# Decode attention block on one core: part of the K and V loads issued from ScalarE's queue

## The chip, the core and the metric

The kernel runs on one core of a Trainium2 chip. The core has five engines with a queue of instructions each: TensorE (PE, matrix products; PEld are its weight loads), VectorE (DVE), ScalarE (ACT), GpSimd (POOL) and SyncE (SP), which here only issues transfers. 16 DMA engines move data from the chip's memory (HBM) to the on-chip buffer (SBUF, 128 partitions). A transfer is issued by an instruction in the queue of SP, ACT or POOL, which first waits until the destination is free. The metric is the device time of the kernel in microseconds, the median of the runs; lower is better.

## What is computed

One decode step for a batch of 2, model width 512: layer norm, attention of 32 heads of width 128 over 8192 cached keys and values (float32), output projection with residual, then layer norm and an MLP (1792 wide, gelu) with residual. Cut to what matters:

```python
def _A_ref(x, k_cache, v_cache, wq, wo):     # x: (2, 1, 512)
    q = heads(x @ wq)                        # k_cache, v_cache: (2, 32, 8192, 128)
    scores = einsum("bhqd,bhkd->bhqk", q, k_cache) * 128 ** -0.5
    p = softmax(scores)
    o = einsum("bhqk,bhkd->bhqd", p, v_cache)
    return merge(o) @ wo
h = x + _A_ref(layernorm(x), k_cache, v_cache, wq, wo)
return h + mlp(layernorm(h), w1, b1, w2, b2)
```

K and V are 268 MB each, so nearly all of the bytes that the kernel reads are these two caches, each read once.

## The kernel before

The main loop runs over `NI` = 32 iterations: `i` stands for a pair of heads `m = i // 2` and a batch entry `b = i % 2`. Per iteration there is one load of K and one of V, 8.39 MB each: 128 partitions (64 for each of the two heads) with 128 consecutive cache rows, 64 KB, in each partition. `load` (line 70) issues them. Iterations 30 and 31 cut their loads into parts.

Three large buffers of 64 KB per partition (`kv`, `BUFS` = 3) hold the query weights at first, then K and V in turn, and at the end the MLP's weights. While one K is worked on, a V is being read or awaited, and the third buffer is filled.

Work on one K, in four chunks of 32 rows: VectorE multiplies the chunk by the query (`multiply`, line 246); GpSimd adds the upper half of 22 to 32 rows to the lower half (`halve`, line 256; in the last three iterations 12 in the last chunk and more shares for ScalarE); VectorE sums the rows to scores (`sums`, line 266). Only in the last three iterations does ScalarE sum rows (`by_act`, line 260). Then comes the maximum: `row_max` (line 270) on VectorE, a transpose on PE (273), `all_max` (277, 280), and on ScalarE `exps`: `nb` (286) and two exponentials (291). With these, PE multiplies V in 64 matmuls (`values`, line 314), ScalarE copies the result (`gather`, line 320) and PE sums it per head (`head_sum`, line 335). This second half, for iteration `i-1`, runs in iteration `i`, beside the chunks of K of `i`.

Order of the issues on SP. In iteration `i`, V of `i` is issued at the top, ahead of `all_max` and `exps` of `i-1`; K of `i+1` is issued after `values` of `i-1`. Each waits until the earlier contents of its buffer are no longer needed. Loads count from 0: K of `i` is load `2i` and V of `i` is load `2i+1`, up to iteration 29.

The output weights `wo` come in ten groups (`PLAN`): five as plain loads on SP (`load_wo`, line 140), and five as indirect loads issued by POOL (line 145), of 96 partitions with 8 KB each, which leave out blocks of partitions. `behind(m)` and `tc.issue_after` put an instruction behind another one in its engine's queue. ScalarE issues one transfer, the input `x` (line 66).

Of the kernel before, what the change touches and what calls it, by code (L numbers as in the profile page):

```python
# [9 lines left out]
F32 = mybir.dt.float32  # L10
I32 = mybir.dt.int32
BF16 = mybir.dt.bfloat16
AF = mybir.ActivationFunctionType
# [3 lines left out]
P = 128  # L17
# [8 lines left out]
BUFS = 3  # L26
# [11 lines left out]
FAR = 4096  # L38


@with_exitstack
def tile_decode_block(ctx: ExitStack, tc: tile.TileContext, x, k, v, wq, wo, w1, b1, w2, b2, out):
    nc = tc.nc
    B, H, SK, DH = k.shape
# [3 lines left out]
    NS = SK // HP  # L48
    NC = NS // CH
    DC = D // P  # L50
# [3 lines left out]
    NI = NM * B  # L54
    SCALE = DH ** -0.5
# [3 lines left out]
    kv = ctx.enter_context(tc.tile_pool(name="kv", bufs=BUFS))  # L59
# [7 lines left out]

    def load(src, i, parts):  # L70
        m, b = divmod(i, B)
        t = kv.tile([P, NS, DH], F32, name="kv", tag="kv")
        rows = src[b, QG * m:QG * m + QG].rearrange("h (p j) d -> (h p) j d", j=NS)
        for s0, n in parts:
            nc.sync.dma_start(t[:, s0:s0 + n], rows[:, s0:s0 + n])
        return t

    wqt = kv.tile([P, DC, H * DH], F32, name="wqs", tag="kv")
    nc.sync.dma_start(wqt, wq.rearrange("(p r) n -> p r n", r=DC))

    ident = const.tile([P, P], F32, name="ident")
# [13 lines left out]
    for blocks in PLAN:  # L95
        shut = blocks if isinstance(blocks, tuple) else None
        r = WR if shut else blocks
        n = (P - 4 * len(shut or ())) * r
# [13 lines left out]
    for _, _, _, blocks in groups:  # L112
        if blocks and blocks not in index:
# [3 lines left out]
            for p in sorted(set(ends)):  # L117
                if ends.count(p) == 1:
                    if p in blocks:
                        edge, step, first = p, FAR, p  # L120
                    else:
                        edge, step = p, first - p - FAR
                    one = work.tile([P, 1], F32, name="ix1")
# [11 lines left out]
    def load_wo(g, gate=None):  # L135
        r0, n, r, shut = groups[g]
        t = wts.tile([P, WR, D], F32, name="wog")
        wo_g[g] = t
        if not shut:
            nc.sync.dma_start(t[:, :r], wo[r0:r0 + n, :].rearrange("(p r) n -> p r n", r=r))  # L140
            return
        if gate is not None:
            next_of_pool(lambda: nc.gpsimd.tensor_copy(gate0, gate))
        next_of_pool(lambda: nc.gpsimd.memset(t, 0.0))
        next_of_pool(lambda: nc.gpsimd.indirect_dma_start(
            t.rearrange("p r n -> p (r n)"), None, wo_runs, bass.IndirectOffsetOnAxis(index[shut], 0),
            element_offset=r0 * D, bounds_check=n // r - 1, oob_is_err=False))
# [30 lines left out]
    ptz = [pt2[:, j] for j in range(2)]  # L178
# [9 lines left out]
    so2 = [psa.tile([P, 512], F32, name=f"so{j}") for j in range(2)]  # L188
# [49 lines left out]
    ST, MX, MT, GM, GI, LT, RL, SS, OP, TP = {}, {}, {}, {}, {}, {}, {}, {}, {}, {}  # L238
    wl = q2.rearrange("p (e n) -> p e n", e=QG)

    def multiply(i, c):
        if c == 0:
            ST[i] = work.tile([P, NS], F32, name="s", bufs=3)
        qb = qps[i // B][:, i % B, None, :].to_broadcast([P, CH, DH])
        kc = kt[i][:, c * CH:(c + 1) * CH, :]
        return nc.vector.tensor_tensor(kc, kc, qb, op=ALU.mult)  # L246
# [28 lines left out]
    def all_max(i):  # L275
        gm = work.tile([1, QG], F32, name="gm")
        last = nc.vector.tensor_reduce(gm, MT.pop(i).rearrange("o (e p) -> o e p", e=QG), axis=AX.X, op=ALU.max,  # L277
                                       negate=True)
        GM[i] = psm.tile([P, QG], F32, name="sm")
        GI[i] = nc.tensor.matmul(GM[i], ones[:1, :], gm, start=True, stop=True)  # L280
        return last

    def exps(i):
        m, b = divmod(i, B)
        nb = work.tile([P, QG], F32, name="nb")
        nc.scalar.activation(nb, GM.pop(i), AF.Copy, scale=SCALE)  # L286
        LT[m] = lt2[:, m % 2]
        s = ST.pop(i).rearrange("p (u j) -> p u j", j=4)
        for e in range(QG):
            ps = slice(e * HP, (e + 1) * HP)  # L290
            nc.scalar.activation(ptz[i % 2][ps, :, 4 * e:4 * e + 4], s[ps], AF.Exp, bias=nb[ps, e:e + 1], scale=SCALE,  # L291
                                 accum_out=LT[m][ps, 32 * e + b:32 * e + b + 1])

    def total(i):
        m, b = divmod(i, B)
# [14 lines left out]
    def values(i, us=range(NS // 4)):  # L310
        so = so2[i % 2]
        for u in us:
            n = u % NG
            m = nc.tensor.matmul(so[32 * n:32 * n + 4 * QG], ptz[i % 2][:, u, :], vt[i][:, 4 * u:4 * u + 4, :],  # L314
                                 start=(u < NG), stop=(u >= NS // 4 - NG))
        return m

    def gather(i):
        SS[i] = work.tile([P, 512], F32, name="ss", bufs=3)
        return nc.scalar.activation(SS[i], so2[i % 2], AF.Copy)  # L320

    def head_sum(i):
        m, b = divmod(i, B)
# [46 lines left out]
    def behind(m):  # L370
        return tc.issue_after(m.ins)
# [8 lines left out]
    def cut(n):  # L380
        return [(j * NS // n, NS // n) for j in range(n)]

    parts_of = {NI - 2: cut(2), NI - 1: cut(2)}
    kt, vt = {}, {}
    next_load = 0
    free_from = 1
    kt[0] = load(k, 0, cut(1))
    for i in range(NI):
        m, b = divmod(i, B)
        done = i - 1  # L390
        late = i == NI - 1
        if not late:
            if i < NI - 2:
                vt[i] = load(v, i, cut(1))
        else:
            vt[i] = load(v, i, [(0, 64), (64, 32), (96, 24), (120, 8)])
            b1r = rows2[:, 0].rearrange("p r q -> p (r q)")[:, :FN]
            nc.vector.memset(b1r, 0.0)
            b2s = rows2[:B, 1].rearrange("b r q -> b (r q)")
            for e in range(B):  # L400
                nc.sync.dma_start(b1r[WB * e::32], b1.rearrange("(n f) -> n f", n=NG))
            nc.sync.dma_start(b2s, b2[None, :].to_broadcast([B, D]))
        if i > 0:
            last = all_max(done)
            exps(done)
            if not late:
                values(done)
        if i < NI - 1:
            kt[i + 1] = load(k, i + 1, parts_of.get(i + 1, cut(1)))
        if i == NI - 2:  # L410
            vt[i] = load(v, i, cut(1))
            nc.sync.dma_start(wl, wo[HL * DH:, :].rearrange("(h p) n -> p h n", p=P))
        if next_load < len(groups) and i == free_from:
            load_wo(next_load, MX[i - 1][:1, 0:1] if next_load == 0 else None)
            next_load += 1
            free_from = NI
        for c in range(NC):
            if i > 0 and c == 0:
                with behind(last):
                    mul = multiply(i, c)  # L420
            else:
                mul = multiply(i, c)
            ended = [g for g in group_end.get(done // B, ())] if done >= 0 and done % B == B - 1 else []
            with behind(mul):
                if i > 0 and c == 1:
                    inverse(done)
                if i > 0 and c == 2 and done % B == B - 1:
                    for h in range(done // B * QG, done // B * QG + QG):
                        head_out(h)
                if c == 3:  # L430
                    for g in ended:
                        turned(g)
                        free_from = i + 1
            halve(i, c)
            by_act(i, c)
            if i > 0 and c == 0 and not late:
                gather(done)
            with behind(mul):
                if c > 0:
                    sums(i, c - 1, True)  # L440
                sums(i, c, False)
            if late and c == 1:
                spare = psq.tile([P, 512], F32, name="spare", tag="qps")
                awake = stay_awake(8, ST[i][:, :NPOOL[True][0]])
            if i > 0 and c == 0:
                total(done)
            if i > 0 and c == 1 and not late:
                head_sum(done)
            if c == 2:
                for g in ended:  # L450
                    turn(g)
        sums(i, NC - 1, True)
        if b == B - 1 and m % 2 == 1 and m + 1 < NM:
            make_q(m + 1)
        if late:
            with behind(awake):
                last = values(done, range(MOST))
            with behind(last):
                row_max(i)
        else:  # L460
            row_max(i)

    hl = NI - 1
    wt = kv.tile([P, 2, NS * DH // 2], F32, name="ws", tag="kv")
    w1t = wt[:, 0, :DC * F].rearrange("p (c f) -> p c f", c=DC)
    w1v = w1.rearrange("(p c) f -> p c f", c=DC)
    for c in range(0, DC, 2):
# [119 lines left out]
    for c in range(DC):  # L587
        with behind(last):
            for n in range(NG):
                m = nc.tensor.matmul(  # L590
                    pf[32 * n:32 * n + 32], cen[:, c, :], w1t[:, c, n * FN:(n + 1) * FN],
                    start=(c == 0), stop=(c == DC - 1))
# [58 lines left out]
```

## Time and profile before

| what | value |
|---|---|
| median of 3 runs | 1307.79 us (1307.79 to 1307.81) |
| span of the profiled execution | 1305.9 us, so 1.9 us of the median lie around it |
| busy: DVE / POOL / PE / ACT | 932.7 / 494.2 / 446.8 / 98.6 us |
| moved by DMA | 561.50 MB, mean 430 GB/s |
| busy share of the 16 DMA engines by slices | 9 (90% or more) in 39 of 40, 8 in the last |
| one multiply (line 246) | 4415 ns mean, 128 of them |

How to read the rows: in a timeline a row is the start in us, the duration in us, the engine and line, the operation, the tile written and the tiles read, the count, and in brackets how long the engine was idle before and what ended that. "SPq" and "ACTq" are the queues' own instructions, such as DMA issues. A row of waits is the waiting engine and line, whom it waited for, the total in us, how many times, and the longest. A row of DMA issues ends with the median time from the issue to the landing. In a row of windows the columns are the window, its length, then the busy time (and count) of PE, PEld, DVE, ACT and POOL, then the granted PE clock, the share of the DMA engines, and GB/s. A row of DMA queues is the queue, its packets, MB, and the share of the 16 engines' span. In the chain of waits, a row is start, duration and what the time went to.

### The profile page before, as it was taken

The page shows a single profiled execution, that of the slowest core. Times are in us where ns is not written, and L with a number is a line of the kernel's source. Part 1 is how long each engine was busy: PE and PEld are TensorE (multiplying, and loading weights), DVE is VectorE, ACT ScalarE, POOL GpSimd, SP SyncE. Part 2 cuts the span into 40 slices and gives each one's busy share as a digit, 9 for nine tenths or more (in the row PEclk, how much of TensorE's full clock was granted, in tenths as well). Part 3 has the DMA queues.
Part 4 walks back from the last instruction along what each step waited for, and adds up shares of the span by engine and source line. Part 5 has one row for each costly group of instructions (what it writes and reads, how often), then busy time and mean ns, then how long its engine had stood idle before and what let it go on. Part 6 is the DMA issues. An engine that isn't in the chain of part 4 may idle for free.

```text
span 1305.9 us, 7466 instructions
## 1 busy us (share of the span) xinstructions
PE 446.8 (34%) x2934; PEld 130.9 (10%) x2934; DVE 932.7 (71%) x551; ACT 98.6 (8%) x431; POOL 494.2 (38%) x151
## 2 busy tenths in 40 slices
PE   3033313333332334413342232333323334123468
PEld 0001001010010101001010010101001011000113
DVE  3666688757688666787766787666787667797891
ACT  0000000000000000000000000000000000004440
POOL 0433344532344432444332454333444433453330
PEclk9566556766566666656766566666666666566689
DMA  9999999999999999999999999999999999999998
GB/s 418 426 440 428 438 422 444 424 440 426 442 426 440 428 438 428 426 444 430 436 426 438 430 434 436 424 442 424 440 426 432 438 432 436 429 428 429 428 434 351
DMA packets 12727, 561.50 MB, mean 430 GB/s; under 512 B 1568, under 2 KB 1584, under 8 KB 2484
## 3 DMA queue, kind: packets, MB, share of 16 engines
q1 hardware_dynamic: 11968, 557.08, 98.8%
q0 software_dynamic: 720, 3.93, 0.7%
q8 instruction: 23, 0.38, 0.1%
q14 instruction: 12, 0.10, 0.0%
q10 hardware_dynamic: 4, 0.00, 0.0%
HBM read 562.32 MB, written 0.00 MB: 431 GB/s over the span
## 4 chain that ended last, share of the span: by engine, by line
DMA 43%; DVE 24%; issue 14%; PE 12%; POOL 5%; ACT 1%; SPq 0%; POOLq 0%; DVEq 0%
DMA kv<-in_A_k_cache_dram 38%; DVE kv L246 14%; PE so L314 10%; DVE s L266 9%; POOL kv L256 5%; DMA kv<-in_A_v_cache_dram 3%; DMA ws<-in_B_w_dram 1%; ACT pt L291 1%; PE rowacc L367 1%; DVE orow L350 1%; PE sm L280 1%; PE sm L273 0%; DVE gm L277 0%; DVE mx L270 0%; ACT nb L286 0%
## 5 line engine op out<-in xcount | busy, mean ns | idle before, releaser
L246 DVE TENSOR_TENSOR kv<-kv,qps 128x4096 f32<-128x4096 f32 x128 | 562.4, 4415 | 313.8 <-DMA kv<-in_A_k_cache_dram 313.6
L256 POOL TENSOR_TENSOR kv<-kv 128x2048 f32<-128x2048 f32 (+3 forms) x128 | 476.8, 3734 | 754.1 <-DVE kv L246 566.3
L266 DVE TENSOR_REDUCE s<-kv 128x32 f32<-128x2048 f32 (+5 forms) x160 | 325.3, 2066 | 10.9 <-POOL kv L256 10.6
L314 PE MATMUL so<-kv,pt 128*8 128x512 f32 x2048 | 280.8, 709 | 42.7 <-ACT pt L291 37.3
L273 PE MATMUL sm<-ident,mx 128*1 128x128 f32 x32 | 10.9, 340 | 446.0 <-DVE mx L270 446.0
L314 PEld LDWEIGHTS so<-kv,pt 128*8 128x8 f32 x2048 | 56.4, 101 | 239.5 <-issue 194.3
L367 PE MATMUL rowacc<-wog,ot 128*2 128x512 f32 x70 | 50.3, 881 | 64.8 <-DVE ot L365 33.4
L286 ACT ACTIVATE nb<-sm 128x2 f32<-128x2 f32 x32 | 5.5, 172 | 851.4 <-PE sm L280 851.4
L231 PE MATMUL qps<-q,pick 2*64 2x256 f32 x64 | 13.8, 577 | 127.6 <-DVE kv L246 127.6
L273 PEld LDWEIGHTS sm<-ident,mx 128*1 128x1 f32 x32 | 2.5, 79 | 472.5 <-issue 278.0
L358 PE MATMUL sm<-ident,orow 2*128 2x2 f32 x35 | 5.2, 244 | 130.1 <-DVE orow L350 130.1
L320 ACT ACTIVATE ss<-so 128x512 f32<-128x512 f32 x31 | 18.5, 598 | 269.6 <-PE so L314 269.6
L260 ACT ACTIVATE kv<-kv 128x128 f32<-128x128 f32 x114 | 33.5, 295 | 24.2 <-DVE kv L246 21.4
L335 PE MATMUL sm<-ss,selr 128*34 128x128 f32 x240 | 28.7, 273 | 0.0
L291 ACT ACTIVATE pt<-s,nb 64x128 f32<-64x128 f32 x64 | 25.5, 399 | 1.4
L335 PEld LDWEIGHTS sm<-ss,selr 128*34 128x34 f32 x240 | 25.1, 112 | 0.0
L260 ACT ACTIVATION_READ_ACCUMULATOR kv<-kv 128x1 f32 x114 | 21.3, 186 | 0.0
L280 PE MATMUL sm<-gm,ones 1*128 1x2 f32 x64 | 16.6, 326 | 11.9 <-DVE gm L277 11.9
L277 DVE TENSOR_REDUCE gm<-sm 1x2 f32<-1x128 f32 x32 | 8.9, 279 | 16.2 <-PE sm L273 16.2
L231 PEld LDWEIGHTS qps<-q,pick 2*64 2x64 f32 x64 | 5.5, 192 | 136.9 <-DVE kv L246 133.2
L358 PEld LDWEIGHTS sm<-ident,orow 2*128 2x128 f32 x35 | 4.4, 207 | 132.6 <-DVE orow L350 79.9
L367 PEld LDWEIGHTS rowacc<-wog,ot 128*2 128x2 f32 x70 | 6.8, 107 | 97.9 <-issue 64.1
(110 smaller groups left out, 169.2 us busy)
## 6 DMA issues: line engine op xcount, KB each, us to landing
kv<-in_A_k_cache_dram SPq DMA_DIRECT2D x4, 4096.0 KB, 32.9
ws<-in_B_w_dram SPq DMA_DIRECT2D x3, 1792.0 KB, 18.5
kv<-in_A_v_cache_dram SPq DMA_DIRECT2D x1, 4096.0 KB, 33.4
wog<-in_A_wo_dram SPq DMA_DIRECT2D x3, 1024.0 KB
kv<-in_A_v_cache_dram SPq DMA_DIRECT2D x1, 2048.0 KB, 37.9
kv<-in_A_v_cache_dram SPq DMA_DIRECT2D x1, 1536.0 KB, 41.2
ws<-in_B_w_dram SPq DMA_DIRECT2D x1, 1024.0 KB, 17.0
wog<-in_A_wo_dram SPq DMA_DIRECT2D x1, 512.0 KB
```

Source lines behind the costliest of these rows:

```text
L231: nc.tensor.matmul(t[e * HP:(e + 1) * HP, :, b], pick[32 * n:32 * n + B, b, :], rows[:, :, e], start=True, stop=True)
L246: return nc.vector.tensor_tensor(kc, kc, qb, op=ALU.mult)
L256: nc.gpsimd.tensor_tensor(t[:, :, :DH // 2], t[:, :, :DH // 2], t[:, :, DH // 2:], op=ALU.add)
L260: nc.scalar.activation(kt[i][:, j, :], kt[i][:, j, :], AF.Copy, accum_out=ST[i][:, j:j + 1])
L266: nc.vector.tensor_reduce(ST[i][:, a:e], kt[i][:, a:e, :d], axis=AX.X, op=ALU.add)
L273: nc.tensor.transpose(MT[i], mx, ident)
L280: GI[i] = nc.tensor.matmul(GM[i], ones[:1, :], gm, start=True, stop=True)
L291: nc.scalar.activation(ptz[i % 2][ps, :, 4 * e:4 * e + 4], s[ps], AF.Exp, bias=nb[ps, e:e + 1], scale=SCALE, accum_out=LT[m][ps, 32 * e + ...
L314: m = nc.tensor.matmul(so[32 * n:32 * n + 4 * QG], ptz[i % 2][:, u, :], vt[i][:, 4 * u:4 * u + 4, :], start=(u < NG), stop=(u >= NS // 4 - ...
L320: return nc.scalar.activation(SS[i], so2[i % 2], AF.Copy)
L335: nc.tensor.matmul(OP[m], sel_row[:, j, B - 1 - c:B - 1 - c + QR], SS[i - 1 + c][:, j * DH:(j + 1) * DH], start=(c == 0 and j == 0), stop= ...
L367: nc.tensor.matmul(rowacc, t[:, r, :], wo_g[g][:, r, :], start=False, stop=(g == len(groups) - 1 and r == n - 1))
```

## The change

Loads 12 to 25 (K of iteration 6 to V of iteration 12) and 38 to 51 (K of 19 to V of 25) are issued by ScalarE; all others stay on SP. In these stretches the issue of K of `i+1` moves to a later place in the program: behind `gather` of `i-1`, in the first chunk of iteration `i`. `next_of_act` fixes ScalarE's order among these issues, `exps` and `gather`. Each large tile now has one of three names in turn with one buffer each, where before one name had three buffers.

```diff
+BY_ACT = [*range(12, 26), *range(38, 52)]
...
+    loads = [0]
+    taken = [0]
+    act_last = [None]
+
+    def next_of_act(make):
+        if act_last[0] is None:
+            act_last[0] = make()
+        else:
+            with tc.issue_after(act_last[0].ins):
+                act_last[0] = make()
+        return act_last[0]
+
+    def kv_tile(shape, name):
+        taken[0] += 1
+        return kv.tile(shape, F32, name=name, tag=f"kv{(taken[0] - 1) % BUFS}", bufs=1)
+
     def load(src, i, parts):
-        t = kv.tile([P, NS, DH], F32, name="kv", tag="kv")
+        t = kv_tile([P, NS, DH], "kv")
...
+        act = loads[0] in BY_ACT
+        loads[0] += 1
         for s0, n in parts:
-            nc.sync.dma_start(t[:, s0:s0 + n], rows[:, s0:s0 + n])
+            if act:
+                next_of_act(lambda: nc.scalar.dma_start(t[:, s0:s0 + n], rows[:, s0:s0 + n]))
+            else:
+                nc.sync.dma_start(t[:, s0:s0 + n], rows[:, s0:s0 + n])
...
-    wqt = kv.tile([P, DC, H * DH], F32, name="wqs", tag="kv")
+    wqt = kv_tile([P, DC, H * DH], "wqs")
...
-        nc.scalar.activation(nb, GM.pop(i), AF.Copy, scale=SCALE)
+        next_of_act(lambda: nc.scalar.activation(nb, GM.pop(i), AF.Copy, scale=SCALE))
...
-        if i < NI - 1:
+        if i < NI - 1 and loads[0] not in BY_ACT:
             kt[i + 1] = load(k, i + 1, parts_of.get(i + 1, cut(1)))
...
             if i > 0 and c == 0 and not late:
                 gather(done)
+            if c == 0 and i < NI - 1 and i + 1 not in kt:
+                kt[i + 1] = load(k, i + 1, parts_of.get(i + 1, cut(1)))
...
-    wt = kv.tile([P, 2, NS * DH // 2], F32, name="ws", tag="kv")
+    wt = kv_tile([P, 2, NS * DH // 2], "ws")
```

The two exponentials in `exps` and the copy in `gather` are wrapped in `next_of_act` in the same way as `nb`.

More of the change, by code (lines that the diff above doesn't have):

```diff
@@ L290, in exps @@
             ps = slice(e * HP, (e + 1) * HP)
-            nc.scalar.activation(ptz[i % 2][ps, :, 4 * e:4 * e + 4], s[ps], AF.Exp, bias=nb[ps, e:e + 1], scale=SCALE,
-                                 accum_out=LT[m][ps, 32 * e + b:32 * e + b + 1])
+            next_of_act(lambda: nc.scalar.activation(
+                ptz[i % 2][ps, :, 4 * e:4 * e + 4], s[ps], AF.Exp, bias=nb[ps, e:e + 1], scale=SCALE,
+                accum_out=LT[m][ps, 32 * e + b:32 * e + b + 1]))
     def total(i):
@@ L319, in gather @@
         SS[i] = work.tile([P, 512], F32, name="ss", bufs=3)
-        return nc.scalar.activation(SS[i], so2[i % 2], AF.Copy)
+        return next_of_act(lambda: nc.scalar.activation(SS[i], so2[i % 2], AF.Copy))
     def head_sum(i):
```

## The prediction

> **What bounds the kernel now.** I read the page's slices and DMA queues first, because both engines that do the arithmetic leave room (VectorE is busy 71% of the span).
>
> ```profile
> span 1305.9 us, 7466 instructions
> DMA  9999999999999999999999999999999999999998
> ...
> q1 hardware_dynamic: 11968, 557.08, 98.8%
> q0 software_dynamic: 720, 3.93, 0.7%
> ```
>
> SyncE's queue q1 alone keeps the 16 DMA engines busy for 98.8% of the span, and POOL's q0 adds 0.7%. The second view is one window from the first transfer to the last landing:
>
> ```profile
> 1.00:1301.80 1300.80, 445.70 (x2911) 130.37 (x2912) 932.46 (x550) 98.57 (x431) 493.71 (x145) 0.66 1.00 432
> ```
>
> The DMA engines have a share of 1.00 in it and move 432 GB/s. The third view is VectorE's timeline: the first multiply of each iteration starts when its K has landed, so these starts are a clock of the stream.
>
> ```profile
> 239.45 8.75 DVE L246 TENSOR_TENSOR kv<-kv,qps 128x4096 f32<-128x4096 f32 x2 [8.32 <-DMA kv<-in_A_k_cache_dram]
> 280.83 8.75 DVE L246 TENSOR_TENSOR kv<-kv,qps 128x4096 f32<-128x4096 f32 x2 [12.25 <-DMA kv<-in_A_k_cache_dram]
> 319.47 8.76 DVE L246 TENSOR_TENSOR kv<-kv,qps 128x4096 f32<-128x4096 f32 x2 [8.27 <-DMA kv<-in_A_k_cache_dram]
> 358.24 8.75 DVE L246 TENSOR_TENSOR kv<-kv,qps 128x4096 f32<-128x4096 f32 x2 [9.58 <-DMA kv<-in_A_k_cache_dram]
> ...
> 515.53 8.75 DVE L246 TENSOR_TENSOR kv<-kv,qps 128x4096 f32<-128x4096 f32 x2 [9.49 <-DMA kv<-in_A_k_cache_dram]
> 554.34 8.75 DVE L246 TENSOR_TENSOR kv<-kv,qps 128x4096 f32<-128x4096 f32 x2 [8.55 <-DMA kv<-in_A_k_cache_dram]
> 595.13 8.75 DVE L246 TENSOR_TENSOR kv<-kv,qps 128x4096 f32<-128x4096 f32 x2 [11.66 <-DMA kv<-in_A_k_cache_dram]
> ...
> 871.58 8.75 DVE L246 TENSOR_TENSOR kv<-kv,qps 128x4096 f32<-128x4096 f32 x2 [9.52 <-DMA kv<-in_A_k_cache_dram]
> 910.05 8.75 DVE L246 TENSOR_TENSOR kv<-kv,qps 128x4096 f32<-128x4096 f32 x2 [9.28 <-DMA kv<-in_A_k_cache_dram]
> ```
>
> Where nothing else is loaded, K follows K after 38.64, 38.77 and 38.81 us, about 38.7. One pair of K and V is 2 x 128 x 64 KB = 16.78 MB, so this is 433.5 GB/s, the rate of the whole window. A load gives each of the 16 engines 8 rows of 64 KB, so a pair is 16 rows for each, and one row takes 38.7 / 16 = 2.42 us. VectorE waits 8 to 12 us for K in every iteration: **the kernel is the time of its bytes on 16 engines that never pause**. An edit changes the end only if it changes the microseconds per byte or empties the queue.
>
> How far the queue is from empty is in the rows of the issues and of SyncE's waits:
>
> ```profile
> kv<-in_A_v_cache_dram SPq DMA_DIRECT2D x31, 30.6
> kv<-in_A_k_cache_dram SPq DMA_DIRECT2D x30, 38.4
> ...
> wog<-in_A_wo_dram,ix POOLq DMA_INDIRECT x5, 26.2
> ```
>
> ```profile
> SPq L75 <- DVE mx L270: 764.5, 28, 29.7
> SPq L75 <- PE sm L301: 175.9, 15, 12.6
> SPq L75 <- PE so L314: 170.4, 15, 13.3
> ```
>
> A load by itself takes 38.7 / 2 = 19.35 us but lands 30.6 (V) or 38.4 us (K) after its issue, so 11 and 19 us of older work lie ahead of it.
>
> **The change, part by part.** Fixed turns of the buffers. The waits show that the old allocation already turned: V loads wait for the end of the scores of the K before (DVE mx, 28 times), K loads for the last use of the V before (PE, 15 + 15 times). With three names in turn, V of iteration i takes the buffer of K of i-1, and K of i+1 that of V of i-1: the same waits. Cost 0. An order that differed only at the first load or the last weights would cost at most the wait there; I see none to price.
>
> Issues on ScalarE. 28 issues leave SyncE and come to ScalarE, at the place where these rows stand for iteration 12:
>
> ```profile
> 504.91 0.33 SPq L75 DMA_DIRECT2D kv<-in_A_v_cache_dram  x1
> ...
> 506.71 0.17 ACT L286 ACTIVATE nb<-sm 128x2 f32<-128x2 f32 x1 [29.11 <-PE sm L280]
> ...
> 517.58 0.33 SPq L75 DMA_DIRECT2D kv<-in_A_k_cache_dram  x1
> 517.59 0.60 ACT L320 ACTIVATE ss<-so 128x512 f32<-128x512 f32 x1 [9.68 <-PE so L314]
> ```
>
> ```profile
> 0.74 0.54 ACTq L66 DMA_DIRECT2D x<-in_A_x_dram  x1
> ```
>
> ScalarE's one issue took 0.54 us, SyncE's usual 0.33. V's wait ends at 504.91, and ScalarE's next instruction, nb, cannot start before 506.71, as it waits for the maximum through VectorE and PE. So 1.80 us cover 0.54 us; behind the wait stand nb and the two exponentials, and values waits for these. If an issue took over 1.80 us, values would start late by the rest, which the slack of the next paragraph takes. K's issue now stands behind the 0.60 us gather, whose wait is the same end of values: 0.60 us later for K, against 19 us of work ahead of it in the queue; behind it ScalarE has nothing until the next nb some 28 us on. 28 x 0.54 = 15 us on an engine busy 8%: 0 on the path. The chain that holds ScalarE's order keeps an order that its program had: 0.
>
> The four changes of queue. Loads 12, 26, 38 and 52 are each K of some iteration, issued on another queue than the V before them, and both then draw on the same engines. Which is served first is not shown for two such loads, but the indirect load by POOL's q0 is nearest: 720 packets are 5 x 144, so 9 for each engine, 8 of them 8 KB of data. If an engine takes one row of 64 KB between two of these, 8 x (2.42 + 0.30) = 21.8 us pass, and 26.2 are shown with the issue of about 1 us and the ends of the path. A queue served first would be through in about 2.4 us, one served last after some 38. So I take turns row by row.
>
> For loads 25 and 26, then (V and K of iterations 12 and 13): V starts at about 515.5, K comes at 517.6, they alternate, and V lands about one row before K, at 554.3 - 2.4 = 552 instead of 504.9 + 30.6 = 535.5.
>
> ```profile
> 547.51 8.61 PE so L314 x64
> 556.12 0.02 issue
> 556.13 38.98 DMA kv<-in_A_k_cache_dram
> ```
>
> Values of iteration 12 starts at 552 instead of 547.5, ends at 560.6, and K of 14 is issued then instead of at 556.1. The queue holds V of 13 (its buffer is free at about 545) and is empty only at 554.3 + 19.4 = 573.7. So 13.1 us of slack remain of 17.6: the stall of values costs 0, and what is late next, the gather, the head sum and the rescaling, comes some 5 us later within an iteration of 38.7 us. By K's next landing the order is the old one. If that cover were gone, the loss would be the idle time of the DMA engines.
>
> The price of the mixing itself is bounded by the same indirect loads. Two of them fall into the steps 239.45 to 280.83 (41.38 us) and 554.34 to 595.13 (40.79):
>
> ```profile
> 232.77 1.16 POOL L145 DMA_INDIRECT wog<-in_A_wo_dram,ix  x1 [0.28 <-POOL wog L144]
> ...
> 547.13 1.01 POOL L145 DMA_INDIRECT wog<-in_A_wo_dram,ix  x1 [0.27 <-POOL wog L144]
> ```
>
> They add 2.7 and 2.1 us. An engine with all its 8 rows of 8 KB has 64 KB to move, 2.42 us; the mean over the engines, 3.93 MB / 5 at 433.5 GB/s, is 1.8 us. Mixing has therefore cost between -0.3 us (2.1 - 2.4) and +0.9 us (2.7 - 1.8) each time. It now happens at four changes of queue and at two direct wo loads, which stay on SyncE while ScalarE's queue streams:
>
> ```profile
> 399.50 0.42 SPq L140 DMA_DIRECT2D wog<-in_A_wo_dram  x1
> ...
> 951.13 0.42 SPq L140 DMA_DIRECT2D wog<-in_A_wo_dram  x1
> ```
>
> Six times: -2 to +5.4 us. Against 2.42 us, the engine that ends last, the two rows give +0.3 and -0.3; I take 0.
>
> Speed of ScalarE's queue. No row has a large load on it. If it ran at the best step of the trace, 38.47 us (871.58 to 910.05), 14 pairs would gain 14 x 0.23 = 3.2 us; the same distance the other way, 38.93, loses 3.2. The engines, the bytes and the 64 KB rows are the same, so I take 0. The Trainium skill, page "DMA: Bandwidth & Descriptors", section "Issuing engines are not separate DMA queues", says that transfers started by different engines share the same 16 DMA engines and that several issuers save issue time alone. By that rule the sum is 0 too, and it speaks against a gain: here the issue time saved, 28 x 0.33 us on SyncE, lies in waits of hundreds of us. No run here shows a large load on ScalarE's queue.
>
> **Sum.** Against the profiled execution: span 1305.9 + (0 buffers) + (0 issues) + (0 late values) + (0 mixing) + (0 pace) = 1305.9. The median, 1307.79, lies 1.9 us above that span. Forecast: **1307.8 us**, its own range 1305.2 to 1310.4 (0.2% each way, which is about what a measurement of this kernel can tell from no change).
>
> **The rivals.** (a) Faster: the slowest of the 16 engines sets each landing, and on ScalarE's queue that engine is less slow. For it: steps between 38.47 and 38.81 us show that the pace isn't quite fixed. Against it: the DMA share is 1.00 already. With 3.2 us from the pace and up to 2 us from mixing: 1307.8 - 3.2 = 1304.6, at best 1302.6. The same page, section "Where 436 GB/s comes from", gives 435.2 GB/s as the ports' ceiling; an estimate by it is 16.78 MB / 435.2 = 38.55 us a pair and a gain of 0.15 x 14 = 2.1 us at most, 1305.7.
>
> (b) Slower by mixing: each of the six costs 0.9 us, 5.4 in all, for 1313.2; half of that, with a pace somewhat worse, is 1311. For it: the step of 41.38 us. Against it: that of 40.79.
>
> (c) Slower by a drained queue: the new queue is served before the old one. K of 13 then takes 517.6 to 537, V of 12 moves for 8 us, V of 13 (issued at 545) goes ahead of its rest, and V of 12 lands at about 573.6. Values ends 8.6 us later, at 582.2, and until then K of 14, and behind it in SyncE's order V of 14, can't be issued: 8.6 us of idle engines at each of four places, 34 us, 1342. It decides once V lands after 573.7 - 8.6 = 565.1. Against it: the 26.2 us of the indirect loads.
>
> (d) The change does not do what it says: the loads still run one after the other, as each issue waits for the other queue. Then all is as before, 1307.8.
>
> **How the numbers follow.** Forecast 0.52, (a) 0.20, (b) 0.17, (c) 0.07, (d) 0.04. Faster by over 0.2% (below 1305.2) is (a), 0.20. Within it are the forecast and (d), 0.56. Slower (above 1310.4) are (b) and (c), 0.24. The range goes from 1303.5, which cuts off the best third of (a), to 1313, which leaves out (c) and the end of (b): some 0.07 below and 0.10 above.
>
> **What would show it.** In the profile after, q10 should hold about 28 x 8.39 = 235 MB and q1 322, with the DMA slices still at 9. Steps between K landings within both stretches should be 38.7 us; 38.5 there says (a), and 38.9 or more the reverse. At the four changes V should land some 17 us later after its issue than the median, values should start about 4.5 us late once, and the next step should be 38.7 again. A step of 47 us there says (c). nb should start 1.8 us after V's issue as before; if it starts later, ScalarE's issue is dearer than 0.54 us. The forecast is wrong if the DMA share falls below 1.00 anywhere, or if the pace of one queue differs from that of the other.

## The result and the profile after

The changed kernel takes 1424.87 us (median of 5 runs, 1423.63 to 1425.41) against 1307.79 us before (median of 5, 1307.72 to 1308.10): a ratio of 1.0894, with a 95% interval of 1.0881 to 1.0908. It is 117 us slower, where no change was forecast. The page of the changed kernel, its first lines, slices and queues:

```profile
span 1422.8 us, 7455 instructions
...
DMA  9999999994999949696999995999959979699998
GB/s 413 440 435 422 439 439 430 432 435 209 442 430 423 442 208 415 283 443 293 419 439 439 421 442 229 442 441 432 430 232 441 433 299 413 293 426 437 427 431 349
...
q1 hardware_dynamic: 7936, 322.20, 52.7%
q10 hardware_dynamic: 4036, 234.89, 38.3%
q0 software_dynamic: 720, 3.93, 0.7%
```

The bytes are where the prediction put them: 235 MB on ScalarE's q10, 322 MB on q1. But eight slices of the DMA row are at 4 to 7: the queue runs empty, in short holes, and between the holes the rate is that of before. By the queues' shares the engines are empty for 8.3% of 1422.8 us, 118 us, against 0.5% of 1305.9, 6.5 us, before: 112 of the 117 us are empty time. So it is issues that come too late, and hardly slower bytes or a slower queue. VectorE's timeline (the same clock of K landings as before; the multiply is now line 269) puts the holes in time:

```profile
319.59 8.75 DVE L269 TENSOR_TENSOR kv<-kv,qps 128x4096 f32<-128x4096 f32 x2 [8.63 <-DMA kv<-in_A_k_cache_dram]
374.62 8.75 DVE L269 TENSOR_TENSOR kv<-kv,qps 128x4096 f32<-128x4096 f32 x2 [21.53 <-DMA kv<-in_A_k_cache_dram]
...
494.55 8.75 DVE L269 TENSOR_TENSOR kv<-kv,qps 128x4096 f32<-128x4096 f32 x2 [8.77 <-DMA kv<-in_A_k_cache_dram]
552.03 8.75 DVE L269 TENSOR_TENSOR kv<-kv,qps 128x4096 f32<-128x4096 f32 x2 [22.68 <-DMA kv<-in_A_k_cache_dram]
624.03 8.75 DVE L269 TENSOR_TENSOR kv<-kv,qps 128x4096 f32<-128x4096 f32 x2 [41.71 <-DMA kv<-in_A_k_cache_dram]
694.48 8.75 DVE L269 TENSOR_TENSOR kv<-kv,qps 128x4096 f32<-128x4096 f32 x2 [10.90 <-DMA kv<-in_A_k_cache_dram]
```

Up to K of 7 (319.59, before 319.47) nothing is lost; both queues have been mixed once by then. K of 8 comes after 55.0 us instead of 38.8, K of 12 after 57.5 instead of 38.8: 16.3 and 18.7 us. K of 13 lands at 624.03 (K of 14 follows without a wait), and K of 15, at 694.48, is 60.6 us later than before (633.84), when it was 36.5 us at K of 12 (552.03 against 515.53). So the end of the stretch loses another 24.1. The second stretch repeats it (14.5, 18.4 and some 24). That is 16.3 + 18.7 + 24.1 + 14.5 + 18.4 + 24 = 116 of the 117 us.

**First kind of hole: PE.** PE's timeline of the changed kernel around K of 8 (254 is `make_q`, 338 `values`), and ScalarE's rows at its end:

```profile
311.01 0.58 PE L303 MATMUL sm<-gm,ones 1*128 1x2 f32 x2 [1.25 <-DVE gm L300]
341.89 1.97 PE L254 MATMUL qps<-q,pick 2*64 2x256 f32 x8 [30.31 <-DVE kv L269]
343.79 8.78 PE L338 MATMUL so<-kv,pt 128*8 128x512 f32 x64
```

```profile
352.65 0.60 ACT L344 ACTIVATE ss<-so 128x512 f32<-128x512 f32 x1 [39.83 <-PE so L338]
352.66 0.33 ACTq L96 DMA_DIRECT2D kv<-in_A_k_cache_dram  x1
```

In the kernel before, PE and SyncE had these rows at the same place (231 is `make_q`, 314 `values`):

```profile
313.12 9.69 PE L314 MATMUL so<-kv,pt 128*8 128x512 f32 x64 [1.29 <-ACT pt L291]
341.78 1.97 PE L231 MATMUL qps<-q,pick 2*64 2x256 f32 x8 [18.97 <-DVE kv L246]
```

```profile
322.88 0.33 SPq L75 DMA_DIRECT2D kv<-in_A_k_cache_dram  x1
```

`make_q` now stands ahead of `values` of 6 in PE's queue. It refills a query buffer that the multiplies of iteration 7 still read, so it waits 30.31 us for VectorE's last one, and `values`, whose operands are there, waits behind it. K of 8 needs the buffer that `values` reads, and is issued at 352.66 instead of 322.88. One row of windows shows the DMA engines meanwhile (share 0.15, 50 GB/s), the next row the same place before K of 12 (0.07), and the third a hole of the second kind:

```profile
338.00:354.00 16.00, 11.26 (x75) 2.87 (x75) 10.19 (x6) 1.00 (x3) 3.72 (x2) 0.71 0.15 50
515.00:530.00 15.00, 12.47 (x75) 3.01 (x75) 8.24 (x6) 0.77 (x2) 1.81 (x1) 0.67 0.07 22
568.00:582.00 14.00, 0.87 (x6) 0.61 (x7) 13.62 (x11) 0.00 (x0) 6.26 (x2) 0.50 0.22 75
```

**Second kind of hole: SyncE**, the third row above. SyncE's timeline at the end of the first stretch:

```profile
580.23 0.33 SPq L98 DMA_DIRECT2D kv<-in_A_v_cache_dram  x1
580.72 0.33 SPq L98 DMA_DIRECT2D kv<-in_A_k_cache_dram  x1
```

V of 13 is issued ahead of K of 13. V's buffer is free only once K of 12 has been worked on (28 us after its landing at 552.03); K's had been free since about 540, and K, which is needed first, waits behind V.

No line of the diff names PE or moves a V ahead of a K. The programs as built do: this is the order of the instructions in the two queues, as the traces have it (line numbers left out), before on the left.

```
PE:  sm<-gm,ones                 sm<-gm,ones
     so<-kv,pt  (values)         qps<-q,pick  (make_q)
     qps<-q,pick  (make_q)       so<-kv,pt  (values)
SP:  ... K12, V12, K13, V13      ... V5, wo, V13, K13, K14
```

The order on PE is changed so at four places (iterations 7, 11, 19, 23), that on SP at the end of each stretch. VectorE's has a third change: the reciprocal and the rescaled rows of `head_out` stand between the row maximum (`row_max`) and its reduction (`all_max`) in seven iterations, in four of them with the copy of `turned` and, on PE, the products with `wo` behind it. The build arranges each engine's queue itself, except where a line such as `issue_after` fixes it; that it does so by when it takes loads to be done is argued, not shown.

### The profile page after: what moved, and what is told of

It reads as the page before. It is cut to its first block, busy times and chain, and to the rows that moved or that the text cites. A ratio compares the mean times of both kernels' runs of the same rounds, so it can differ in the third digit from the quotient of the medians.

```text
span 1422.8 us, 7455 instructions
## 1 busy us (share of the span) xinstructions
PE 438.6 (31%) x2934; PEld 130.0 (9%) x2934; DVE 932.3 (66%) x551; ACT 98.6 (7%) x431; POOL 494.7 (35%) x151
## 4 chain that ended last, share of the span: by engine, by line
DMA 39%; DVE 30%; issue 14%; PE 8%; POOL 6%; another core or an unknown queue 2%; ACT 1%; SPq 0%; POOLq 0%; DVEq 0%; ACTq 0%
DMA kv<-in_A_k_cache_dram 32%; DVE kv L269 17%; DVE s L289 12%; PE so L338 7%; DMA kv<-in_A_v_cache_dram 6%; POOL kv L279 6%; DMA ws<-in_B_w_dram 1%; ACT pt L314 1%; PE qps L254 1%; DVE orow L374 0%; PE sm L303 0%; PE sm L296 0%; DVE mx L293 0%; DVE gm L300 0%
## 5 line engine op out<-in xcount | busy, mean ns | idle before, releaser
L338 PE MATMUL so<-kv,pt 128*8 128x512 f32 x2048 | 275.0, 695 | 42.9 <-ACT pt L314 30.9
L254 PE MATMUL qps<-q,pick 2*64 2x256 f32 x64 | 13.8, 576 | 162.1 <-DVE kv L269 162.1
L167 POOL MEMSET wog<- 128x2048 f32 x5 | 9.0, 1805 | 29.1 <-PE rowacc L391 29.1
```

Source lines behind the costliest of these rows:

```text
L254: nc.tensor.matmul(t[e * HP:(e + 1) * HP, :, b], pick[32 * n:32 * n + B, b, :], rows[:, :, e], start=True, stop=True)
```

## The experiments

Theory 1 is that the orders cost the time. Its rivals are the second queue itself (B) and the parts of the change alone.

**The turns alone.**

```diff
-BY_ACT = [*range(12, 26), *range(38, 52)]
+BY_ACT = []
```

> The fixed turns of the buffers alone, every load on SyncE. Theory 1 (the instruction orders that came with the change cost the time, not the queues or the turns): 1307.8 us, within 0.5. Rival A (the turns take part in it, by another wait of a load): 1312 or more.

1307.64 us, ratio 1.0 (0.9991 to 1.001), the order on every engine as before. The turns cost nothing.

**PE held.**

```diff
-                values(done)
+                read = values(done)
...
-            make_q(m + 1)
+            with tc.issue_after(read.ins):
+                make_q(m + 1)
```

> The changed kernel, with each make_q held behind the values matmuls before it on PE. Theory 1: the K landings after the four places where make_q (line 254) stood ahead of values came 16.3, 18.7, 14.5 and 18.4 us late; these 68 us go, the late K after each stretch (24 us twice) stays: 1357 us, 1350 to 1365. Rival B (two queues on the same engines are what costs: mixing, or a slower ScalarE queue): 1415 to 1425, since no load moves to another queue.

1357.19 us: the 68 us went and nothing else. K lands every 38.6 to 38.8 us through the first stretch, but for one step of 41.1 with a `wo` load (before, the next step had it), and the steps of 72.2 and 70.4 us at the ends of the two stretches stay.

**SyncE held.** Each SyncE load of K, V and `wo` is put behind the one before it in the program (`next_of_sp`, made like `next_of_act`).

```diff
-                nc.sync.dma_start(t[:, s0:s0 + n], rows[:, s0:s0 + n])
+                next_of_sp(lambda: nc.sync.dma_start(t[:, s0:s0 + n], rows[:, s0:s0 + n]))
```

> The changed kernel, with SyncE's loads held in the order of the program, so that K of 13 and of 26 are issued ahead of V of 13 and of 26; make_q still ahead of values. Theory 1: the two ends of the stretches give back 24 us each, 68 us stay: 1377 us, 1368 to 1386. Rival B: 1415 to 1425.

1381.11 us, 4 us above the number but within the bounds: the ends of the stretches gave back 44 us, not 48.

**Both held.** The two edits together.

> Both holds at once; 28 loads still on ScalarE's queue, four changes of queue. VectorE's order keeps one change: the rescaled rows of head_out and the copies of turned stand between the row maximum and its reduction over partitions, about 6 us ahead of values in some iterations. Theory 1: 1307.8 us if the 13 to 17 us of slack take these 6 us and the mixing of two queues is free; up to 1316 if not. Rival B: above 1390.

1307.74 us, ratio 1.0 (0.9991 to 1.001). All 117 us are gone, with 28 loads still on ScalarE's queue. This is the kernel that the prediction had worked out, so its steps can be read here, in the queues, in PE's timeline at the first change of queue, in a window of the first stretch, and at its end in PE's row of `values` of 12 and SyncE's issue of K of 14:

```profile
q1 hardware_dynamic: 7936, 322.20, 57.2%
q10 hardware_dynamic: 4036, 234.89, 41.6%
```

```profile
276.08 9.68 PE L348 MATMUL so<-kv,pt 128*8 128x512 f32 x64 [6.98 <-DMA kv<-in_A_v_cache_dram]
```

```profile
280.00:515.00 235.00, 75.34 (x508) 22.05 (x504) 172.61 (x79) 10.50 (x36) 92.52 (x25) 0.64 1.00 433
```

```profile
553.46 7.05 PE L348 MATMUL so<-kv,pt 128*8 128x512 f32 x64 [1.29 <-ACT pt L324]
```

```profile
560.57 0.33 SPq L108 DMA_DIRECT2D kv<-in_A_k_cache_dram  x1
```

`values` of 5 waits 6.98 us for its V, which shared the engines with K of 6 and landed 46 us after its issue, and starts at 276.08, 5.6 us later than before (270.50); K of 6 still lands 41.55 us after K of 5, the step of before (41.38). The DMA share in the stretch is 1.00 at 433 GB/s, and VectorE's changed order, which is still there, costs nothing. One more thing changed with the hold on PE: `make_q` now runs right behind `values` (at 321.12 in iteration 7) without a wait for VectorE, so it refills another query buffer. The kernel before has that wait, 18.97 us behind `values`, and loses nothing by it.

**One swap in the kernel before, on PE.** The converse: no second queue, `values` of 6 behind the `make_q` that the buffer of iteration 7 is refilled by.

```diff
-            if not late:
+            if not late and i != 7:
                 values(done)
...
+        if i == 7:
+            first = make_q(m + 3)
+            with behind(first):
+                values(done)
+            kt[i + 1] = load(k, i + 1, cut(1))
+            gather(done)
```

(K of 8 and `gather` are left out at their old places in iteration 7, and `make_q` in iteration 11.)

> The kernel before, every load on SyncE, with one swap: in iteration 7 the make_q that refills the second query buffer stands ahead of values of 6 on PE (and K of 8 and gather of 6 after it in the program). Theory 1: make_q waits for the last multiply of iteration 7, 22 us after K of 7 lands; with 2 and 9 us for make_q and values K of 8 is issued at 33 us, lands 19.4 + 2 us later at 55 instead of 38.8, and the end is 16 us later: 1324 us, 1320 to 1328. Rival C (the swap costs only because V came late on a mixed queue): under 1312.

1321.43 us, 13.8 us slower. PE's timeline shows the same wait, and SyncE's the late issue of K of 8 and, behind it, V of 8:

```profile
341.75 1.97 PE L231 MATMUL qps<-q,pick 2*64 2x256 f32 x8 [29.95 <-DVE kv L247]
343.64 9.81 PE L315 MATMUL so<-kv,pt 128*8 128x512 f32 x64
```

```profile
347.50 0.33 SPq L75 DMA_DIRECT2D kv<-in_A_k_cache_dram  x1
353.52 0.33 SPq L75 DMA_DIRECT2D kv<-in_A_v_cache_dram  x1
```

K of 8 was issued 5 us sooner than the expectation had it, and ahead of the end of `values` (353.45): its issue waits for VectorE's semaphore and comes with the row maximum of iteration 7 (347.51), while V of 8 waits for PE's. The two have exchanged buffers, K of 8 taking that of K of 7. So the edit changed more than the order on PE. The run shows that a K issued 24.6 us late costs 13.8 us with one queue; it does not show the path of the changed kernel, where K waits for `values`.

**One swap in the kernel before, on SyncE.** On top of the turns, V of 13 ahead of K of 13, all on SyncE.

```diff
+            if i == 13:
+                vt[i] = load(v, i, cut(1), 1)
+                with tc.issue_after(sp_last[0].ins):
+                    kt[i] = load(k, i, cut(1), -1)
```

(The last argument keeps each load in the buffer that it had; K of 13 is left out in iteration 12.)

> The kernel before with fixed turns, every load on SyncE, and one swap: V of 13 is issued ahead of K of 13. Theory 1: K of 13 waits until K of 12 has been worked on, as after the first stretch of the changed kernel, and the end is 24 us later: 1332 us, 1326 to 1338. Rival C: the queue's other loads cover it, under 1316.

1335.09 us, 27.5 us slower. V of 13 is issued at 544.87, when K of 12 has been worked on, and K of 13 right behind it. Here the swap alone costs its time with one queue, so the second queue isn't needed for this kind of loss; for the first kind the evidence is the kernel with PE held.

**The later place of K alone.**

```diff
-                next_of_act(lambda: nc.scalar.dma_start(t[:, s0:s0 + n], rows[:, s0:s0 + n]))
+                (lambda f: f())(lambda: nc.sync.dma_start(t[:, s0:s0 + n], rows[:, s0:s0 + n]))
```

> The changed kernel with its 28 loads issued by SyncE instead of ScalarE; K of the next iteration keeps its later place in the program. Theory 1 (the second queue is what turned the orders; here PE, VectorE, ScalarE and GpSimd keep the order of before, and on SyncE two wo loads go ahead of a K): 1307.7 us, within 1. Rival D (the later place of K is enough): 1340 or more.

1307.62 us. The later place alone turns only the two `wo` loads, and costs nothing.

**One stretch, and four loads.**

```diff
-BY_ACT = [*range(12, 26), *range(38, 52)]
+BY_ACT = [*range(12, 26)]
```

The second kernel has `[12, 13, 14, 15]`.

> The change with the first stretch alone (loads 12 to 25 on ScalarE), nothing held. Theory 1: make_q ahead of values twice (16.3 and 18.7 us) and V of 13 ahead of K of 13 once (24.1): 1307.7 + 59.1 = 1366.8 us, 1362 to 1372. Rival B (cost by load on ScalarE's queue, 117 / 28 = 4.2 us each): 14 loads give the same 1366, so this run tells of adding up and not between these two.

> Four loads alone on ScalarE (12 to 15: K and V of iterations 6 and 7), nothing held. The order has one make_q ahead of values (of iteration 6) and V of 8 ahead of K of 8 on SyncE. Theory 1: both swaps hold up the same K of 8, so they overlap: between the larger one, 24 us, and their sum, 40: 1332 to 1348 us. Rival B (4.2 us for each load on ScalarE's queue): 1324.5.

1369.71 and 1334.15 us. One stretch costs 62.1 us, about half of 117. Four loads cost 26.5 us, 6.6 for each, where the stretch has 4.4 and the whole change 4.2: the loss goes by swaps, not by loads. Four loads in a row are enough to turn the order on PE and on SyncE.

**The pace of ScalarE's queue.** Both held, and `BY_ACT = range(4, 58)`.

> PE and SyncE held in order, loads 4 to 57 on ScalarE: 27 pairs, for the pace of that queue. Theory 1 with equal pace: 1307.7 us, within 2. A pace of 38.47 us per pair would give 1301.5, one of 38.93 would give 1313.9.

1307.87 us, ratio 1.0002 (0.9992 to 1.0011). The window over 940 us of it:

```profile
160.00:1100.00 940.00, 291.55 (x1911) 85.17 (x1904) 690.88 (x319) 41.05 (x139) 381.35 (x108) 0.64 1.00 433
```

The two queues have the same pace: the records of the single transfers give a median of 2420 ns for a row of 64 KB on either.

**Two queues at work all through.** Both held, and V of 6 to 28 on ScalarE beside K on SyncE (`BY_ACT = range(13, 58, 2)`).

> PE and SyncE held in order, and V of iterations 6 to 28 on ScalarE while every K stays on SyncE, so that two queues are at work all through, not at four places. Theory 1 with mixing at no cost: 1307.7 us, within 2. Rival B with the prediction's upper price of 0.9 us for each mixing, some 45 of them: 1345 or more.

1344.74 us, ratio 1.0297 (1.0275 to 1.0318): theory 1 as far as it called steady mixing free is wrong here. Rival B's 1345 is the number that came, but its reason does not hold, as the following shows. The page:

```profile
span 1342.3 us, 7468 instructions
...
q1 hardware_dynamic: 8656, 364.14, 62.9%
q10 hardware_dynamic: 3316, 192.94, 33.8%
q0 software_dynamic: 720, 3.93, 0.8%
```

The queues are busy for 97.5% of 1342.3, 1309 us, against 99.5% of 1305.9, 1299 us, before: 9 us more at work, 27 us more empty. The 9 us are not rows made dearer by the mixing: in the records of the single transfers a row of 64 KB takes 2418 ns here on either queue and 2420 before (medians). What is longer are the first rows after the queue has run empty, by 0.56 to 0.75 us on each engine, and it runs empty, or nearly so, some eleven times between 318 and 1137 us. The landings of K show why: they come 48 to 53 and 30 to 32 us apart by turns, as K and V share the engines; the next V waits until the late K has been worked on (V of 7 is issued at 319.78, into a hole from 318.96 to 320.75). To test this:

**Halves of each load on both queues.** Both held, and `BY_ACT = range(12, 52)`.

```diff
             if act:
-                next_of_act(lambda: nc.scalar.dma_start(t[:, s0:s0 + n], rows[:, s0:s0 + n]))
+                h = n // 2
+                next_of_sp(lambda: nc.sync.dma_start(t[:, s0:s0 + h], rows[:, s0:s0 + h]))
+                next_of_act(lambda: nc.scalar.dma_start(t[:, s0 + h:s0 + n], rows[:, s0 + h:s0 + n]))
```

> Every load from 12 to 51 cut into two halves, rows 0 to 63 of each partition on SyncE's queue and 64 to 127 on ScalarE's, PE and SyncE held in order. Two queues are at work all through, as with V on ScalarE and K on SyncE (1344.7 us), but here both halves of a load land together and the loads land one after another. Theory E (that kernel lost its time because K and V, taking turns, land late, so that the work on them starts late and the next issue comes after the queue has run empty): 1307.7 us, up to 1310. Theory F (taking turns between two queues itself costs the DMA engines): 36 us over 23 pairs there, 1.6 a pair; 20 pairs here: 1340; with only the busy time that grew there, 9.5 us or 0.4 a pair: 1316.

1323.74 us, ratio 1.0121 (1.0104 to 1.0138), above theory E's 1310 and above theory F's smaller price (1316), below its larger one (1340). Its queues:

```profile
span 1322.2 us, 7565 instructions
...
q1 hardware_dynamic: 11968, 389.31, 68.6%
q10 hardware_dynamic: 5764, 167.78, 29.5%
q0 software_dynamic: 720, 3.93, 0.7%
```

98.8% of 1322.2 is 1306 us: 7 us more at work, 9 us more empty. The loads do not land one after another everywhere, as theory E had taken them to: four K landings (6, 10, 16 and 24) come 48.6 to 51.3 us after the one before, each where SyncE's queue had a piece that ScalarE's had not (the whole V of 5, or a plain `wo` load). Around the K landing behind each, the DMA share falls to 0.77 to 0.85 for 12 to 14 us, together 10 us: this is the empty time. Of the 7 us, some 2.6 are the first rows after these four holes (0.61 to 0.66 us each), and some 3.4 come from the pieces: two of 32 KB take 2433 ns where a row of 64 KB takes 2422 (means without the long first rows). So theory F is out: rows do not get dearer by taking turns. Theory E's mechanism holds, late landings and an emptied queue, but its 1310 took for granted that the halves stay level. That the extra piece on SyncE is what put them out of step is read from the order of the issues and not tested by a run.

## Why the prediction was wrong

**The bound** was read rightly: the bytes on 16 engines that never pause, with 11 and 19 us of queued work ahead of an issue. So was its rule that an edit costs what it empties the queue by: 112 of the 117 us are empty time, and the other 5 are the first rows after the eight large holes, each 0.55 to 0.73 us longer on every engine.

**The step that failed** stands in the part on the issues: K waits for "the same end of values: 0.60 us later for K", and "The chain that holds ScalarE's order keeps an order that its program had: 0". Both look at ScalarE's queue alone. The order on PE and SyncE was taken from the profile before, at no cost and without a reason, though the diff fixes ScalarE's order alone. `make_q` went ahead of `values` at four places, so that K of 8, for one, was issued 29.8 us later (352.66 against 322.88) and not 0.60; and V went ahead of K at two, so that K of 13 was issued at 580.72 with its buffer free since about 540. 1357.19 and 1381.11 us with one kind held, 1307.74 with both, show that this is the whole loss. Why the build chose these orders stays open. That they would turn could not be seen in the trace of before; what a turn costs could: VectorE's last multiply ends 22 us after K lands, `make_q` and `values` take 11, so K's issue comes 33 us after a landing instead of 3.4, and the work queued ahead takes only some 13 of these 30.

**The other terms.** Turns: 0 forecast, 1307.64 measured. Issues on ScalarE: 0 forecast; they take 0.33 to 0.39 us there, not the 0.54 of the one row before, and the cover holds (with both held, nb follows V's issue of 504.98 by 1.79 us). Late values: with both held the start is at 553.46 and K's issue at 560.57, where 552 and 560.6 were forecast, but that is luck. `values` waited there for the exponentials, which the changed order on VectorE and PE made late, and not for V. The wait for V that was forecast came at the first change of queue (6.98 us), and there too the end does not move. Mixing: 0 taken, right for four changes and two `wo` loads. The upper price of 0.9 us gave 1345 for steady mixing by luck too: those 37 us are an emptied queue and first rows behind it, not dearer rows. Pace: 0 taken, 1307.87 over 27 pairs. The Trainium skill's rule on the page "DMA: Bandwidth & Descriptors", section "Issuing engines are not separate DMA queues", that several issuers save issue time alone, agrees with these 1307.87 us.

**The rivals.** (a) has nothing for it. (b) is refuted: the six mixings cost nothing here, and steady mixing loses its time by late landings. (c) named the sign that came, idle engines because K and V were issued late and a step far above 38.7, but by a cause that is not there: a queue drained first. It was given 0.07 and a price of 34 us. (d) is out: q10 moved its 235 MB, and with both held V of 5 landed 46 us after its issue, beside K of 6, and not after 30.6.

## What to carry to other kernels

Where a build arranges the queues, an edit on one engine can turn the order on the others: before pricing anything by the trace, list each engine's order in both programs, and fix with an explicit edge those neighbours of which one waits long. An instruction that refills a buffer early is dangerous ahead of one that frees a buffer which a load is waiting for. And a stream that runs at its ceiling with some 13 us of slack loses nothing for a late piece of 5 us, and what is beyond the slack otherwise: K of 8 was issued 29.8 us late and landed 16.3 us late. Loads that take turns on two queues all land late, which uses up that slack.

## What had not been expected of the hardware

Two queues on the same 16 DMA engines have the same rate one after the other (433 GB/s on either), and cost nothing when they meet four times. When both are in use all through, a row of 64 KB still takes the same 2.42 us, yet the kernel takes 16 to 37 us more, as loads that take turns land late and the queue runs empty. After each time that it ran empty, the first rows took 0.55 to 0.75 us longer on every engine: of the 117 us of this change some 5 are such restarts.
